# A transformer block's modulation weights with nine neighbouring rows per partition, and its condition vector loaded as columns

## The chip, the cores and the metric

One Trainium2 chip, one core. The metric is the device time of one execution in microseconds (us). "PE" is TensorE's matmul side, "DVE" VectorE, "ACT" ScalarE, "POOL" GpSimd, "SP" the engine that issues most loads.

## The reference

One block of a diffusion transformer: B = 2, 256 tokens each, D = 1152, all in bfloat16. What matters here is that a condition vector c (2 x 1152) is turned into six modulation vectors by one matmul with w_mod (1152 x 6912), and that layer norm of x does not need c.

```python
mod = (silu(c) @ w_mod).reshape(B, 6, 1, D)
shift_a, scale_a, gate_a, shift_m, scale_m, gate_m = [mod[:, i] for i in range(6)]
h = layernorm(x) * (1 + scale_a) + shift_a
qkv = (h @ wqkv).reshape(B, N, 3, H, Dh)
# ... attention, wo, second layernorm with scale_m / shift_m, gelu MLP ...
```

## The kernel before

The kernel is a list of operations that a scheduler written in Python puts in order per engine. PE and SP keep program order; for the start, ACT and DVE orders are fixed by hand. The parts that matter here:

```python
wmod_v = w_mod.rearrange("(k p) f -> p k f", p=P)      # row k*128+p on partition p
# loads of the head, in SP's order; c on ACT's queue
dma(CSB[0:18, :], c.rearrange("b (k p) -> (b k) p", p=P), ..., "ld_c", eng="act")   # 18 rows of 256 bytes
for b in range(2):
    dma(X[:, 2*b:2*b+2, :], xv[b], ...)                 # x0, x1: runs of 4608 bytes
for (ka, kb) in ((0, KC), (KC, KT)):                    # KC = 4, KT = 9
    for k0, k1 in ((0, 3), (3, 6), (6, 9)):             # scale columns: 3 + 3 loads, runs of 1024 / 1280 bytes
        dma(WSC[:, k0:k1, ka*P:kb*P], wmod_v[:, k0:k1, D+ka*P:D+kb*P], ...)
    for kt in range(ka, kb):
        dma(WK[:, kt, :], wqkv_v[:, kt, D:2*D], ...)
# ...
for i in range(5):                                       # warm-up matmuls
    mm(ps32(5), IDENT, Q4B, True, True)
tr(CT_PS, CSB[0:18, :], IDENT[0:18, 0:18])               # c rows -> columns on TensorE
act(... e.activation(out=TH, in_=CT_PS, func=Tanh, scale=0.5) ..., "c_tanh")
dve(... e.tensor_scalar(out=HC, in0=CT_PS, scalar1=0.5, op0=mult) ..., "c_half")
dve(... e.scalar_tensor_tensor(out=ST, in0=TH, scalar=1.0, in1=HC, op0=add, op1=mult) ..., "c_silu")
# ... first layer norm, its transposes, the first scale columns, the k projection of kt 0 to 3 (blocks of 128 of D's 1152) ...
for kt in range(KT):                                     # second scale columns: need the LAST of the six loads
    mod_kt(WSC, kt, 0, "scb_%d" % kt, (KC, KT))
sc1a(KC, KT)                                             # DVE copies those scales out of PSUM
# ...
S.first = {
    "dve": ["zq4b", "c_half", "c_silu", "bn_ln1_1_0", "bn_ln1_1_1", "bn_ln1_1_2", "aggr_ln1_1", "veps_ln1_1", "bn_ln1_2_0",
            "xn_1", ...],                                # c's work stands AHEAD of layer norm
    "act": ["ld_c", "c_tanh", "sum_ln1_0", "sq_ln1_0", ...],
}
```

Of the kernel before, what the change touches and what calls it, by code (L numbers as in the profile page):

```python
# [496 lines left out]
ALU = mybir.AluOpType  # L497
ACTF = mybir.ActivationFunctionType
AX = mybir.AxisListType

P = 128
# [43 lines left out]
def build_kernel(nc, x, c, wqkv, wo, w_mod, w_fc1, w_fc2, out):  # L545
    S = Sched()
# [4 lines left out]
    with (  # L551
# [4 lines left out]
        def sb(off, nbytes, dt=BF16):  # L556
            assert off % 4 == 0 and off + nbytes <= ARENA_BYTES, (off, nbytes)
            v = arena[:, off // 2:(off + nbytes) // 2]
            if dt == F32:
                v = v.bitcast(F32)  # L560
            return v

        def ps32(bank, c0=0, n=512):
            return psum[:, bank * 512 + c0: bank * 512 + c0 + n]

        def ps16(bank, c0=0, n=1024):
            v = psum[:, bank * 512: (bank + 1) * 512].bitcast(BF16)
            return v[:, c0:c0 + n]
# [15 lines left out]
        def misc(nbytes):  # L584
            o = mo[0]
            mo[0] += (nbytes + 3) // 4 * 4
            assert mo[0] <= ARENA_BYTES
            return o
# [41 lines left out]

        IDENT = sb(misc(256), 256)
        ONES = sb(misc(256), 256)
        CSB = sb(misc(256), 256)
        TH = sb(misc(72), 72, F32)
        HC = sb(misc(72), 72, F32)
        ST = sb(misc(36), 36)
# [26 lines left out]
        xv = x.rearrange("b (p t) d -> b p t d", t=2)  # L663
        outv = out.rearrange("b (p t) d -> b p t d", t=2)
        wqkv_v = wqkv.rearrange("(k p) f -> p k f", p=P)
        wmod_v = w_mod.rearrange("(k p) f -> p k f", p=P)
        wo_v = wo.rearrange("(k p) f -> p k f", p=P)
        wfc1_v = w_fc1.rearrange("(k p) f -> p k f", p=P)
        wfc2_v = w_fc2.rearrange("(k p) f -> p k f", p=P)
# [1 line left out]
        def dma(dst, src, nbytes, name, is_out=False, eng="sp", run=4096):  # L671
            eff = 0.95 if run >= 4096 else (1.0 if run >= 2304 else (1.08 if run >= 1536 else 1.14))
            return S.op(eng, 500.0 if eng == "sp" else 150.0, lambda e: e.dma_start(dst, src), reads=[src], writes=[dst],  # L673
                        name=name, dma_bytes=nbytes * eff, is_out=is_out)

        def dve(cost, fn, reads, writes, name):
            return S.op("dve", cost, fn, reads=reads, writes=writes, name=name)

        def act(cost, fn, reads, writes, name):
            return S.op("act", cost, fn, reads=reads, writes=writes, name=name)  # L680
# [10 lines left out]
        def mm(o, l, r, st, sp, **kw):  # L691
            S.instr(lambda e: e.matmul(o, lhsT=l, rhs=r, start=st, stop=sp, **kw), reads=[l, r], writes=[o])  # L692

        def tr(o, i_, idn):
            S.instr(lambda e: e.transpose(o, i_, idn), reads=[i_, idn], writes=[o])  # L695


        dma(CSB[0:18, :], c.rearrange("b (k p) -> (b k) p", p=P), 18 * 256, "ld_c", eng="act")
        for b in range(2):
            dma(X[:, 2 * b:2 * b + 2, :], xv[b], 2 * P * D * 2, "ld_x%d" % b)  # L700
        for (ka, kb) in ((0, KC), (KC, KT)):
# [22 lines left out]
        for i in range(5):  # L724
            S.unit("pe", 430.0, "warm_a%d" % i)
            mm(ps32(5), IDENT, Q4B, True, True)
        CT_PS = ps16(6, 0, 18)
        S.unit("pe", 100, "c_T")
        tr(CT_PS, CSB[0:18, :], IDENT[0:18, 0:18])
        act(200, lambda e: e.activation(out=TH, in_=CT_PS, func=ACTF.Tanh, scale=0.5), [CT_PS], [TH], "c_tanh")  # L730
        dve(170, lambda e: e.tensor_scalar(out=HC, in0=CT_PS, scalar1=0.5, scalar2=None, op0=ALU.mult), [CT_PS], [HC], "c_half")
        i3 = IDENT.rearrange("p (a i) -> p i a", a=4)
        dve(200, lambda e: e.tensor_reduce(out=QS, in_=i3, axis=AX.X, op=ALU.add), [IDENT], [QS], "qs")
        q4 = QS.unsqueeze(1).broadcast_to([P, 4, 32])
# [22 lines left out]
        for t in range(4):  # L757
# [3 lines left out]
            else:  # L761
# [3 lines left out]
                                                                                 op0=ALU.subtract, op1=ALU.mult),  # L765
# [480 lines left out]
        for t in range(4):  # L1246
            b = t // 2
# [48 lines left out]
def bass_standalone__dit_block__diffusion_kernel(  # L1296
    nc: bass.Bass,
    x: bass.AP,
    c: bass.AP,
    wqkv: bass.AP,  # L1300
    wo: bass.AP,
    w_mod: bass.AP,
    w_fc1: bass.AP,
    w_fc2: bass.AP,
    out: bass.AP,
):
    build_kernel(nc, x, c, wqkv, wo, w_mod, w_fc1, w_fc2, out)
# [28 lines left out]
```

## Time and profile before

| | before |
|---|---|
| time, median of 3 runs (range) | 245.71 us (245.51 to 245.8) |
| span of the profiled run | 243.9 us |
| PE busy | 239.0 us, 98% |
| PE's waits in the whole run | 1.5 us at the start, 0.4 us near 18.7 us |

From the page of the before kernel: busy time by engine, the DMA packets, the queue that carries c (q10), and the chain of work that ended last.

```profile
span 243.9 us, 4070 instructions
...
PE 239.0 (98%) x1755; PEld 147.4 (60%) x1755; DVE 120.9 (50%) x218; ACT 66.5 (27%) x134; POOL 21.3 (9%) x39
...
DMA packets 30140, 51.59 MB, mean 212 GB/s; under 512 B 1703, under 2 KB 15787, under 8 KB 30123
...
q10 hardware_dynamic: 27, 0.00, 0.0%
...
PE psum L692 90%; DMA arena<-in_w_mod_dram 5%; SPq L673 2%; PE psum L695 1%; DVE arena L1259 0%; DVE arena L1260 0%
```

The kernel is bound by PE; L692 is the helper that issues every matmul, L695 the one that issues transposes. The view of waits for PE, "who waited for whom, total us, times, longest":

```profile
PE psum L692 <- POOL arena L715: 1.5, 1, 1.5
PE psum L692 <- DMA arena<-in_w_mod_dram: 0.4, 1, 0.4
```

Those are all of PE's waits. The critical chain in order of time (start, length, what) shows where the second comes from:

```profile
7.11 11.57 DMA arena<-in_w_mod_dram
18.68 0.05 issue
18.73 40.89 PE psum L692 x310
```

A load of w_mod, the last of the six scale loads, is issued at 7.11 us and lands at 18.68; from then on the chain is PE work up to the last two DVE operations. So 0 to 18.7 us ("the head") is the one stretch where a load or c's path can move the time. The timeline of the head, cut to c's work and the first layer-norm work (start, length, engine, line, operation; in brackets the idle time before it and what ended it):

```profile
0.79 0.59 ACTq L673 DMA_DIRECT2D arena<-in_c_dram  x1
...
3.75 0.19 PE L695 MATMUL psum<-arena 18*128 18x18 bf16 x1
...
3.98 0.19 ACT L730 ACTIVATE arena<-psum 128x18 f32<-128x18 bf16 x1 [1.28 <-PE psum L695]
4.27 0.18 DVE L731 TENSOR_SCALAR arena<-psum 128x18 f32<-128x18 bf16 x1 [3.09 <-ACT arena L730]
...
4.41 1.16 ACT L751 ACTIVATE arena<-arena 128x1152 bf16<-128x1152 bf16 x1 [0.24 <-DMA arena<-in_x_dram]
4.49 0.18 DVE L736 SCALAR_TENSOR_TENSOR arena<-arena 128x18 bf16<-128x18 f32 x1
4.58 1.47 DVE L743 BATCH_NORM_STATS2 arena<-arena 128x6 f32<-128x384 bf16 x3
```

c's work (transpose, tanh L730, halving L731, product L736) ends 0.26 us after ACT has x at 4.41 us, so it costs layer norm at most 0.17 us. The load of c itself had landed by 2.2 us; its transpose stood behind warm-up matmuls in PE's order until 3.75. PE's timeline of the end of the head:

```profile
13.04 5.33 PE L692 MATMUL psum<-arena 128*128 128x256 bf16 x71
18.73 14.45 PE L692 MATMUL psum<-arena 128*128 128x2 bf16 x163 [0.35 <-DMA arena<-in_w_mod_dram]
```

PE starts its run of projections of kt 0 to 3 at 13.04 us, is through with what it can do at 18.37 and waits 0.35 us for the load. That is the slack of everything ahead of it on PE.

### The profile page before, as it was taken

The numbers are of one execution on the slowest core, as the hardware profiler recorded it, in microseconds if no ns is written. First come the engines' busy times: TensorE is split into PE (matmuls) and PEld (weight loads), VectorE is DVE, ScalarE is ACT, GpSimd is POOL, SyncE is SP. The second block draws the span as 40 slices with busy tenths as digits, with TensorE's granted clock in tenths as the row PEclk, the third lists the DMA queues.
The fourth block names the chain that finished last, engine by engine and source line by source line (L and its number), as shares of the span: only waits on it lengthen the run. The fifth ranks groups of instructions, "written<-read, shape, count | busy, mean of one in ns | idle before, by whom it ended". The sixth has DMA issues, their size and how long they took to land.

```text
span 243.9 us, 4070 instructions
## 1 busy us (share of the span) xinstructions
PE 239.0 (98%) x1755; PEld 147.4 (60%) x1755; DVE 120.9 (50%) x218; ACT 66.5 (27%) x134; POOL 21.3 (9%) x39
## 2 busy tenths in 40 slices
PE   7999999999999999999999999999999999999994
PEld 2698754556667666898444444444656565656584
DVE  3814398596997899689999500000022211111112
ACT  5730340345424206973233222223000000000000
POOL 1400000000021186400000000020000000000000
DMA  6999999999995999979953498030000000000000
GB/s 234 333 381 391 389 392 389 398 411 409 389 350 171 343 390 392 393 264 393 312 173 86 145 329 300 0 86 14 0 16 19 16 16 19 16 27 21 19 16 19
DMA packets 30140, 51.59 MB, mean 212 GB/s; under 512 B 1703, under 2 KB 15787, under 8 KB 30123
## 3 DMA queue, kind: packets, MB, share of 16 engines
q1 hardware_dynamic: 29680, 50.14, 57.5%
q0 software_dynamic: 416, 1.19, 1.6%
q8 instruction: 14, 0.23, 0.4%
q14 instruction: 3, 0.02, 0.0%
q10 hardware_dynamic: 27, 0.00, 0.0%
HBM read 50.14 MB, written 1.19 MB: 210 GB/s over the span
## 4 chain that ended last, share of the span: by engine, by line
PE 91%; DMA 5%; SPq 2%; issue 0%; DVE 0%
PE psum L692 90%; DMA arena<-in_w_mod_dram 5%; SPq L673 2%; PE psum L695 1%; DVE arena L1259 0%; DVE arena L1260 0%
## 5 line engine op out<-in xcount | busy, mean ns | idle before, releaser
L692 PE MATMUL psum<-arena 128*128 128x384 bf16 (+12 forms) x1666 | 235.8, 308 | 1.9 <-POOL arena L715 1.5
L692 PEld LDWEIGHTS psum<-arena 128*128 128x128 bf16 (+4 forms) x1666 | 142.2, 97 | 91.3 <-issue 4.7
L1054 DVE SCALAR_TENSOR_TENSOR arena<-arena 128x1152 f32<-128x1152 bf16 x32 | 44.7, 1413 | 0.6
L1259 DVE TENSOR_TENSOR arena<-psum,arena 128x384 f32<-128x384 f32 (+3 forms) x14 | 7.0, 500 | 68.0 <-PE psum L692 68.0
L1168 ACT ACTIVATE arena<-psum 128x512 bf16<-128x512 f32 (+1 forms) x44 | 22.4, 520 | 42.7 <-PE psum L692 42.7
L687 ACT ACTIVATE arena<-psum 128x512 bf16<-128x512 f32 (+6 forms) x35 | 19.0, 560 | 39.8 <-PE psum L692 39.1
L689 DVE CAST arena<-psum 128x512 bf16<-128x512 f32 (+3 forms) x14 | 8.9, 645 | 11.9 <-PE psum L692 11.9
L673 POOL DMA_DIRECT2D dit_scratch<-arena x3 | 1.8, 616 | 115.9 <-DVE arena L689 59.1
L1136 POOL TENSOR_TENSOR arena<-arena 128x384 f32<-128x384 f32 x12 | 10.9, 914 | 11.2 <-DVE arena L1135 9.6
L1081 DVE CAST arena<-psum 72x32 bf16<-72x32 f32 x1 | 0.2, 188 | 21.3 <-PE psum L692 21.3
L743 DVE BATCH_NORM_STATS2 arena<-arena 128x6 f32<-128x384 f32 (+1 forms) x18 | 9.5, 548 | 0.1
L1141 ACT ACTIVATE arena<-arena 128x1152 bf16<-128x1152 f32 x4 | 5.3, 1343 | 11.1 <-DVE arena L1140 11.1
L1135 DVE TENSOR_TENSOR arena<-psum,arena 128x384 f32<-128x384 f32 x12 | 6.5, 552 | 1.5 <-PE psum L692 1.4
L1260 DVE TENSOR_TENSOR arena<-arena 128x384 bf16<-128x384 f32 (+3 forms) x14 | 7.0, 501 | 0.5
L695 PE MATMUL psum<-arena 128*128 128x128 bf16 (+1 forms) x89 | 7.1, 219 | 0.0
L695 PEld LDWEIGHTS psum<-arena 128*128 128x128 bf16 (+1 forms) x89 | 5.8, 98 | 2.0 <-issue 0.8
L1158 ACT ACTIVATE arena<-psum,arena 128x128 bf16<-128x128 bf16 x16 | 6.0, 456 | 1.7 <-PE psum L695 1.1
L1155 DVE TENSOR_SCALAR arena<-psum,arena 128x128 bf16<-128x128 bf16 x20 | 5.4, 335 | 1.9 <-PE psum L695 1.9
L1061 DVE TENSOR_REDUCE arena<-arena 128x36 f32<-128x1152 f32 x4 | 5.4, 1346 | 0.0
L1058 DVE STREAM_TRANSPOSE arena<-arena 128x1152 f32<-128x1152 f32 x4 | 5.4, 1363 | 0.0
L984 ACT ACTIVATE arena<-psum,arena 128x256 bf16<-128x256 f32 x8 | 3.7, 472 | 1.3 <-PE psum L692 0.9
L980 DVE TENSOR_REDUCE arena<-psum 128x2 f32<-128x512 f32 x4 | 2.8, 689 | 1.8 <-PE psum L692 1.8
(47 smaller groups left out, 45.2 us busy)
## 6 DMA issues: line engine op xcount, KB each, us to landing
arena<-in_w_fc_dram SPq DMA_DIRECT2D x9, 1152.0 KB, 7.6
arena<-in_w_fc_dram SPq DMA_DIRECT2D x4, 2592.0 KB, 17.5
arena<-in_wqkv_dram SPq DMA_DIRECT2D x18, 288.0 KB, 10.2
arena<-in_w_mod_dram SPq DMA_DIRECT2D x3, 1728.0 KB, 20.2
arena<-in_w_mod_dram SPq DMA_DIRECT2D x3, 864.0 KB, 13.8
arena<-in_w_mod_dram SPq DMA_DIRECT2D x9, 288.0 KB, 10.5
arena<-in_wqkv_dram SPq DMA_DIRECT2D x1, 2592.0 KB, 16.6
arena<-in_wo_dram SPq DMA_DIRECT2D x1, 2592.0 KB, 24.4
```

The costliest lines, as they stand in the source:

```text
L673: return S.op(eng, 500.0 if eng == "sp" else 150.0, lambda e: e.dma_start(dst, src), reads=[src], writes=[dst], name=name, dma_bytes=nbyte ...
L687: act(c_act(n), lambda e: e.activation(out=dst, in_=src, func=ACTF.Copy), [src], [dst], name)
L689: dve(c_dve_psum16(n) if psum16 else c_dve_psum32(n), lambda e: e.tensor_copy(dst, src), [src], [dst], name)
L692: S.instr(lambda e: e.matmul(o, lhsT=l, rhs=r, start=st, stop=sp, **kw), reads=[l, r], writes=[o])
L695: S.instr(lambda e: e.transpose(o, i_, idn), reads=[i_, idn], writes=[o])
L743: dve(550, lambda e, s=s, o=o: e.bn_stats(out=o, in_=s), [s], [o], "bn_%s_%d" % (tag, ci))
L1054: dve(1270, lambda e, w=w, s=s, acc=acc: e.scalar_tensor_tensor(out=acc, in0=w, scalar=s, in1=acc, op0=ALU.mult, op1=ALU.add), [w, s, acc] ...
L1135: dve(550, lambda e, o=o, ga=ga, x1c=x1c: e.tensor_tensor(out=x1c, in0=o, in1=ga, op=ALU.mult), [o, ga], [x1c], "wo_t1_%d_%d" % (t, ci))
L1136: S.op("pool", 930, lambda e, xs=xs, x1c=x1c: e.tensor_tensor(out=x1c, in0=x1c, in1=xs, op=ALU.add), reads=[x1c, xs], writes=[x1c], name=" ...
L1168: act(c_act(ntok), lambda e: e.activation(out=dst, in_=o, func=ACTF.Gelu_apprx_tanh), [o], [dst], "gelu_%d_%d" % (f, tok0))
L1259: dve(c_dve_psum32(w), lambda e, o=o, gm=gm, t1=t1: e.tensor_tensor(out=t1, in0=o, in1=gm, op=ALU.mult), [o, gm], [t1], "fc2_t1_%d_%d" % ( ...
L1260: dve(c_dve_32(w), lambda e, t1=t1, x1c=x1c, ost=ost: e.tensor_tensor(out=ost, in0=t1, in1=x1c, op=ALU.add), [t1, x1c], [ost], "fc2_out_%d ...
```

## The change

Its intent: c comes onto the partitions directly, without a transpose on PE and its PSUM detour. For that, partition p must hold rows 9p to 9p+8 of w_mod, nine neighbours in DRAM, so that c's nine elements of a partition lie side by side too.

```diff
-        wmod_v = w_mod.rearrange("(k p) f -> p k f", p=P)
+        wmod_v = w_mod.rearrange("(p k) f -> p k f", p=P)
...
-        dma(CSB[0:18, :], c.rearrange("b (k p) -> (b k) p", p=P), 18 * 256, "ld_c", eng="act")
+        dma(CSB.rearrange("p (b k) -> p b k", b=2), c.rearrange("b (p k) -> p b k", p=P), 18 * 256, "ld_c", eng="act")
...
-        CT_PS = ps16(6, 0, 18)
-        S.unit("pe", 100, "c_T")
-        tr(CT_PS, CSB[0:18, :], IDENT[0:18, 0:18])
-        act(200, lambda e: e.activation(out=TH, in_=CT_PS, func=ACTF.Tanh, scale=0.5), [CT_PS], [TH], "c_tanh")
-        dve(170, lambda e: e.tensor_scalar(out=HC, in0=CT_PS, scalar1=0.5, scalar2=None, op0=ALU.mult), [CT_PS], [HC], "c_half")
+        act(200, lambda e: e.activation(out=TH, in_=CSB, func=ACTF.Tanh, scale=0.5), [CSB], [TH], "c_tanh")
+        dve(100, lambda e: e.tensor_scalar(out=HC, in0=CSB, scalar1=0.5, scalar2=None, op0=ALU.mult), [CSB], [HC], "c_half")
```

(The tile CSB shrinks from 256 to 36 bytes a partition.) Each load of w_mod still takes a slice of columns, so no two rows join into a longer run.

More of the change, by code (lines that the diff above doesn't have):

```diff
@@ L632, in build_kernel @@
         ONES = sb(misc(256), 256)
-        CSB = sb(misc(256), 256)
+        CSB = sb(misc(36), 36)
         TH = sb(misc(72), 72, F32)
```

## The prediction

> **What bounds the kernel now.** TensorE. The profiled span is 243.9 us and the page gives PE 239.0 us busy (98%). The chain that ended last is PE matmuls (L692) without a break from 18.73 us to 241 us. The view of waits gives PE two waits in the whole run: 1.5 us at the start and 0.35 us ending at 18.73 us, for a load of w_mod. Before that, the chain runs through SP's issues into an 11.57 us w_mod transfer issued at 7.11 us. So only in the head, 0 to 18.7 us, can loads or the c path move the time. There the DMA engines are full: the table by stretches shows a DMA share of 0.92 to 1.1 from 3 us on.
>
> **What the change does.**
> 1. w_mod rows go to partitions as nine neighbours instead of 128 apart. A load still takes column slices of a row, so runs stay 1024, 1280, 2304 and 4608 bytes and the packets stay as many. I expect the same packet times (medians 46, 57, 95 and 182 ns). The first 1024-byte loads run at about 280 GB/s (5 to 9 us), mean packet 54 ns against a median of 46; if neighbouring rows removed that tail, 1152 x 8 ns / 16 engines = 0.6 us of DMA time would go. I give that a small chance.
> 2. c: 18 packets of 256 bytes become 256 of 18 bytes. The old ones took 15 to 18 ns. At that price the new load needs about 256 x 17 / 16 = 0.27 us of every DMA engine, against 0.02 before, and pushes the load that PE awaits at 18.7 us by about 0.25 us (estimates). The Trainium skill ("DMA: Bandwidth & Descriptors", Specifications) says that transfers below 512 bytes miss line rate; no run shows yet what 18 bytes cost.
> 3. Removed: one transpose (0.19 us on PE) among warm-up matmuls. tanh started at 3.98 us, the halving at 4.27, the product at 4.49, VectorE's first layer-norm statistics at 4.58 us, although x had landed at 4.41. If c lands before 4 us, VectorE starts about 0.15 us earlier. But the same page (Queues, rings and completion order) says that an engine takes turns between rings packet by packet. c's 16 packets an engine could alternate with the x packets (178 ns and more) and land near 5 us. ACT and VectorE have the c work ahead of layer norm, so the statistics would start 0.5 to 1 us later. PE's slack is 0.35 us.
>
> **Sum.** A gain in the head beyond the 0.35 us wait is lost; a DMA delay shows fully. -0.1 (chance of faster rows, shorter chain) +0.25 (c packets) +0.1 (chance of a late c) gives about +0.2 us: 245.9 us, range 245.2 to 246.8. Faster by over 2%: 0.01; within 2%: 0.98; slower: 0.01.
>
> **What would show it.** Packets under 512 bytes rise by about 245; w_mod packet medians stay; PE's wait near 18.7 us remains or grows to 0.4 to 0.7 us, or tanh is late and PE's first 18 us shift; after it PE runs without a gap and takes the same 222 us to the last matmul.
>
> **What would make it wrong.** The row order changes HBM speed: PE's wait goes (at best -0.4 us), or new PE waits for w_mod appear up to 60 us, where DMA is full too. 18-byte packets cost several times 17 ns: +1 us and more. The instruction order on VectorE or ACT is made from modelled times; another order could open small PE waits anywhere.

## The result

The after kernel took 245.86 us (median of 4 runs, 245.81 to 245.99), the before kernel 245.74 us (4 runs, 245.51 to 245.8) beside it. The ratio is 1.0007, 95% interval 0.999 to 1.0025: the same. The prediction said 245.9, range 245.2 to 246.8.

The page after, the same lines as before; line numbers are lower by 3 from L731 on (L730 is now L727):

```profile
span 244.3 us, 4059 instructions
...
PE 238.5 (98%) x1744; PEld 147.1 (60%) x1754; DVE 120.9 (50%) x218; ACT 66.4 (27%) x134; POOL 21.2 (9%) x39
...
DMA packets 30385, 51.59 MB, mean 211 GB/s; under 512 B 1948, under 2 KB 16032, under 8 KB 30368
...
q10 hardware_dynamic: 272, 0.00, 0.1%
...
PE psum L692 92%; PE psum L695 2%; DMA arena<-in_c_dram 2%; DVE arena L740 1%; DVE arena L761 1%; POOL arena L744 0%; POOL arena L752 0%; DVE arena L806 0%; DVE arena L741 0%; DVE arena L1256 0%; ACT arena L727 0%; DVE arena L1257 0%; DVE a
```

There are 245 packets more, all under 512 bytes: c's 18 + 9 became 256 + 16 (data and semaphore writes). The w_mod load is gone from the chain, and c's load has come in. The view of waits for PE, after:

```profile
PE psum L692 <- POOL arena L715: 1.5, 1, 1.5
PE psum L692 <- DVE arena L741: 0.3, 1, 0.3
```

PE no longer waits for w_mod at all. Its other wait, for a layer-norm step (L741, the aggregation), ends at 6.97 us, well before the projections; in the second profile of this kernel (e8 below) it is absent. The critical chain of after in order of time:

```profile
0.79 3.92 DMA arena<-in_c_dram
4.74 0.23 ACT arena L727
5.01 0.06 issue
5.07 0.18 DVE arena L733
5.25 1.40 DVE arena L740 x3
6.68 0.25 DVE arena L741
...
7.19 0.58 POOL arena L744
7.79 0.58 DVE arena L761
```

The load of 4.5 KB now opens the chain: it is issued at 0.79 us and releases tanh at 4.74. The timeline of the head, after:

```profile
0.79 0.46 ACTq L673 DMA_DIRECT2D arena<-in_c_dram  x1
...
4.74 0.22 ACT L727 ACTIVATE arena<-arena 128x18 f32<-128x18 bf16 x1 [2.17 <-DMA arena<-in_c_dram]
4.74 0.18 DVE L728 TENSOR_SCALAR arena<-arena 128x18 f32<-128x18 bf16 x1 [3.55 <-DMA arena<-in_c_dram]
4.86 1.15 ACT L748 ACTIVATE arena<-arena 128x1152 bf16<-128x1152 bf16 x1
...
5.07 0.18 DVE L733 SCALAR_TENSOR_TENSOR arena<-arena 128x18 bf16<-128x18 f32 x1 [0.15 <-ACT arena L727]
5.17 1.47 DVE L740 BATCH_NORM_STATS2 arena<-arena 128x6 f32<-128x384 bf16 x3
```

The chain of c is shorter by a transpose, yet it ends 0.58 us later (product at 5.07 against 4.49), because ACT waits 2.17 us and DVE 3.55 us for c. Both have c's work ahead of layer norm in their fixed order, so the statistics start at 5.17 instead of 4.58. And PE's end of the head:

```profile
13.45 0.28 PE L695 MATMUL psum<-arena 128*128 128x128 bf16 x2
13.56 19.65 PE L692 MATMUL psum<-arena 128*128 128x256 bf16 x232
```

The projections start at 13.56, 0.52 us later, and run on without a gap: the load is there when PE comes to it. The packets of the trace say why c is late (start times in us; each row 18-byte packets of c as listed by the trace, which does not name the DMA engine). Packet times in this document and in its expectations are 0.3 us later than on the clock of the views, where c's first packet starts at 1.75 us before and at 2.85 after; the shift is the same in every run, so differences between packet times stand:

```
before: 18 c packets of 256 bytes   first start 2.06, last end 2.19; x's first packet 2.13
after: 256 c packets of 18 bytes    first start 3.16, last end 4.52; x's first packet 2.12
  starts in after: 3.641 3.650 3.658 3.666 3.686 | 3.821 3.830 3.838 3.846 3.865
  a packet of x lasts 0.178
```

The first row of starts comes back 0.180 us later, one x packet apart. An 18-byte packet lasts only 0.009 us. Until x's first load is through, the records alternate in this way, one of c and one of x; after that the rest of c follows in bursts.

### The profile page after: what moved, and what is told of

It is laid out like the page before. It is cut to its first block, busy times and chain, and to the rows that moved or that the text cites. A ratio compares the mean times of both kernels' runs of the same rounds, so it can differ in the third digit from the quotient of the medians.

```text
span 244.3 us, 4059 instructions
## 1 busy us (share of the span) xinstructions
PE 238.5 (98%) x1744; PEld 147.1 (60%) x1754; DVE 120.9 (50%) x218; ACT 66.4 (27%) x134; POOL 21.2 (9%) x39
## 4 chain that ended last, share of the span: by engine, by line
PE 94%; DVE 2%; DMA 2%; issue 1%; POOL 0%; ACT 0%; DVEq 0%
PE psum L692 92%; PE psum L695 2%; DMA arena<-in_c_dram 2%; DVE arena L740 1%; DVE arena L761 1%; POOL arena L744 0%; POOL arena L752 0%; DVE arena L806 0%; DVE arena L741 0%; DVE arena L1256 0%; ACT arena L727 0%; DVE arena L1257 0%; DVE arena L733 0%; DVE arena L796 0%; DVE arena L743 0%
## 5 line engine op out<-in xcount | busy, mean ns | idle before, releaser
L692 PE MATMUL psum<-arena 128*128 128x384 bf16 (+10 forms) x1656 | 234.8, 307 | 2.5 <-POOL arena L715 1.5
L695 PE MATMUL psum<-arena 128*128 128x128 bf16 x88 | 7.1, 219 | 0.1
L695 PEld LDWEIGHTS psum<-arena 128*128 128x128 bf16 x88 | 5.6, 98 | 1.8 <-DVE arena L761 0.9
```

Of the source, the lines that this page charges most:

```text
L692: S.instr(lambda e: e.matmul(o, lhsT=l, rhs=r, start=st, stop=sp, **kw), reads=[l, r], writes=[o])
L695: S.instr(lambda e: e.transpose(o, i_, idn), reads=[i_, idn], writes=[o])
```

## The experiments

**The theories.** *Late c*: the only thing that moves the time is c's late landing, which holds up layer norm; the row order does nothing. *Two effects*: the new rows speed the head's loads by about 0.5 us (in the after profile the last 1280-byte packet of the scale loads ended at 17.91 us, before at 18.48), and the late c eats the gain. *Small packets*: the DMA time of 256 packets is what costs. Four runs came first: each half of the change alone, and a reordering that hides the late c, on both kernels.

### e1_rows_only: the row order alone

```diff
 (on the before kernel; result wrong on purpose, since c stays in the old order)
-        wmod_v = w_mod.rearrange("(k p) f -> p k f", p=P)
+        wmod_v = w_mod.rearrange("(p k) f -> p k f", p=P)
```

> The before kernel with the new row order of w_mod alone; c stays in the old order, so the result is wrong on purpose. Late-c theory (the new rows do nothing; only the late c moves the time): 245.7 us, as before; the last 1280-byte packet of w_mod ends near 18.5 us and PE waits about 0.35 us near 18.7. Two-effects theory (the rows speed the head's loads by about 0.5 us and the late c eats it): the last 1280-byte packet ends near 17.9 to 18.0 us, PE's wait at 18.7 is gone, 245.3 to 245.4 us. Either way tanh stays at about 4.0 us.

Measured: 245.64 us (5 runs, 245.03 to 245.97), ratio to before 0.9996, interval 0.9982 to 1.0009. Wrong result. The last 1280-byte packet ended at 18.81 us, later than before. PE's wait in its view of waits:

```profile
PE psum L692 <- DMA arena<-in_w_mod_dram: 0.7, 1, 0.7
```

In this profile the new rows alone did not bring the load forward, which speaks against the two-effects theory. It does not settle it: the interval reaches down to 0.4 us faster, and one landing proves little, as the next runs show.

### e2_c_only: the c columns alone

```diff
 (on the after kernel; result wrong on purpose)
-        wmod_v = w_mod.rearrange("(p k) f -> p k f", p=P)
+        wmod_v = w_mod.rearrange("(k p) f -> p k f", p=P)
```

> The after kernel with the old row order of w_mod; result wrong on purpose. Both theories: tanh at about 4.7 us, first statistics near 5.2 us, 245.8 to 246.0 us. They differ in the load: two-effects theory has the last 1280-byte packet end at 18.5 us or later, so PE waits again at 18.7 to 18.9 us for about 0 to 0.2 us; late-c theory has it at 17.9 us as in the after run.

Measured: 245.93 us (245.42 to 246.02), ratio 1.0001, interval 0.9989 to 1.0014; wrong result. The halving started at 4.58 us and the statistics at 5.01, so c is late with the old rows too. The last 1280-byte packet ended at 18.76 us and PE waited 0.27 us for it. Neither theory's picture is complete: the load landed at 17.9 or 18.8 us without regard to the rows.

### e3_ln_first and e4_before_ln_first: layer norm ahead of c's work

```diff
-            "dve": ["zq4b", "c_half", "c_silu", "bn_ln1_1_0", "bn_ln1_1_1", "bn_ln1_1_2", "aggr_ln1_1", "veps_ln1_1", "bn_ln1_2_0",
+            "dve": ["zq4b", "bn_ln1_1_0", "bn_ln1_1_1", "bn_ln1_1_2", "aggr_ln1_1", "veps_ln1_1", "c_half", "bn_ln1_2_0", "c_silu",
                     "xn_1", ...
-            "act": ["ld_c", "c_tanh", "sum_ln1_0", "sq_ln1_0", ...
+            "act": ["ld_c", "sum_ln1_0", "c_tanh", "sq_ln1_0", ...
```

> The after kernel with ACT and VectorE doing the first layer-norm work before the c work, so that c's late landing is hidden. Statistics start at about 4.4 us and xn_T near 8.2 us. Late-c theory: 245.6 to 245.75 us, PE waits again for w_mod at 18.7 us. Two-effects theory: 245.3 to 245.4 us, no PE wait between 9 and 19 us above 0.1 us. If the small packets' DMA time were what costs, the time would stay at 245.9 us.

> The before kernel with the same reordering of ACT and VectorE. Both theories: no gain, 245.7 us, since PE has 0.35 us of slack to the w_mod load at 18.7 us; PE's wait there grows a little, to 0.35 to 0.5 us. If the layer-norm chain did bound the head, it would be 0.1 to 0.2 us faster.

Measured: on the after kernel 245.46 us (245.15 to 246.04), ratio to before 0.9993, interval 0.998 to 1.0007. On the before kernel 245.92 us (245.27 to 246.06), ratio 1.0008, interval 0.9995 to 1.0022. Both correct. DVE's timeline and PE's, of the after kernel with layer norm first:

```profile
4.44 1.48 DVE L740 BATCH_NORM_STATS2 arena<-arena 128x6 f32<-128x384 bf16 x3 [3.25 <-DMA arena<-in_x_dram]
```

```profile
13.08 5.33 PE L692 MATMUL psum<-arena 128*128 128x256 bf16 x71
18.62 11.57 PE L692 MATMUL psum<-arena 128*128 128x2 bf16 x138 [0.20 <-DMA arena<-in_w_mod_dram]
```

The statistics start as soon as x is there, PE's projections start at 13.08 (13.04 before the change), and the wait for w_mod is back. The late c is hidden, and the load ends the head again. The median lies below the 245.6 to 245.75 us that the late-c theory gave, but no gain over the before kernel can be told from noise. The profiled run of the latter had the load at 18.02 us and no wait for it, so its wait did not grow as I expected.

### e5_c_behind_x and e6_c_behind_x_ln_first: the suspected delay made larger

```diff
-        dma(CSB.rearrange("p (b k) -> p b k", b=2), c.rearrange("b (p k) -> p b k", p=P), 18 * 256, "ld_c", eng="act")
         for b in range(2):
             dma(X[:, 2 * b:2 * b + 2, :], xv[b], 2 * P * D * 2, "ld_x%d" % b)
+        dma(CSB.rearrange("p (b k) -> p b k", b=2), c.rearrange("b (p k) -> p b k", p=P), 18 * 256, "ld_c")     # on SP's queue
```

(e6 has the reordering of e3 as well; "ld_c" leaves ACT's list.)

> The after kernel with c's column load issued on SP's queue behind the two x loads, so that c lands later still. Late-c theory: the last c packet near 5.9 to 6.1 us, tanh near 6.2 us, statistics near 6.6 us, 2.0 us later than before the change; PE has about 0.35 us of slack to the w_mod load, so about 1.3 to 1.8 us slower than before: 247.0 to 247.6 us, with no PE wait for w_mod. If a late c did not matter: 245.7 to 246.0 us.

> The same late c, but with the first layer-norm work ahead of the c work on ACT and VectorE. Late-c theory: statistics back at 4.4 us, 245.3 to 245.9 us although c lands at 6 us. If it is the placing of c's packets or SP's extra issue that costs, the time stays near that of the run with c behind x and the old order.

Measured: e5 247.81 us (4 runs, 247.3 to 248.22), ratio 1.0084, interval 1.0065 to 1.0102, clearly slower. Its runs fall into two pairs: 247.3 and 247.4 us at a granted clock of 1.0 and 0.998, as the late-c theory expected, and 248.2 us twice at 0.993, above it. e6 246.31 us (4 runs, 245.95 to 246.35), ratio 1.002, interval 1.0007 to 1.0034. Both correct. DVE in e5:

```profile
6.12 0.18 DVE L728 TENSOR_SCALAR arena<-arena 128x18 f32<-128x18 bf16 x1 [4.93 <-DMA arena<-in_c_dram]
6.45 0.18 DVE L733 SCALAR_TENSOR_TENSOR arena<-arena 128x18 bf16<-128x18 f32 x1 [0.16 <-ACT arena L727]
6.55 1.47 DVE L740 BATCH_NORM_STATS2 arena<-arena 128x6 f32<-128x384 bf16 x3
```

The statistics start 1.97 us later than before the change, and the time of the profiled run is 1.66 us longer (247.30 against 245.64), the rest being taken up by PE's slack. With layer norm first, about two thirds of that come back (246.3 us) although c's packets lie in about the same place; that is still above the 245.9 us expected. The rest goes through ACT, whose tanh I had put second and which stood for c here, on the chain that ended last:

```profile
6.45 0.22 ACT L727 ACTIVATE arena<-arena 128x18 f32<-128x18 bf16 x1 [0.90 <-DMA arena<-in_c_dram]
```

### e7_more_small_packets: the price of a small packet

```diff
 (on e3; nobody reads DUM, a memset late on POOL waits for it; two more semaphores)
+        dv, cv = DUM.rearrange("p (k w) -> p k w", w=2)[:, :, 0], wqkv[0:P, 0:18]        # 128 x 18 packets of 2 bytes
+        S.op("act", 150.0, lambda e: e.dma_start(dv, cv, allow_slow_non_contiguous=True), ..., name="ld_dummy")
```

> The after kernel with layer norm first, plus one more load that nobody waits for in the head: 2304 packets of 2 bytes on ACT's queue behind c. It prices small packets. At the 9 ns that an 18-byte packet took in the after run it takes 2304 x 9 / 16 = 1.3 us of each DMA engine, all before the w_mod load that PE waits for at 18.7 us: 1.0 to 1.4 us slower than the run with layer norm first alone, so 246.5 to 247.0 us with a PE wait for w_mod of 1.2 to 1.6 us. At the 15 to 18 ns that my prediction used: 247.6 to 248.0 us. If small packets only fill gaps of the engines: no change, 245.3 to 245.9 us.

Measured: 248.27 us (4 runs, 247.1 to 249.87), ratio 1.0094, interval 1.0045 to 1.0142; correct. Two runs took 247.1 us at a granted clock of 1.0, close to the 246.5 to 247.0 us of the 9 ns theory; two took 249.4 and 249.9 at 0.993. The profile is of the 249.4 us run. The 2304 packets took a mean of 9.02 ns. Of the 1152 packets of the last three scale loads, the middle one ended 1.0 us later than in e3 and the 1050th 1.33 us later (17.71 against 16.38 us), about what 9 ns a packet says; but the very last ended 3.4 us later (21.79 against 18.39). The extra microseconds lie in the last hundred packets. In addition PE waited three times for w_mod and its clock fell. Two rows of the table by stretches (stretch, its length, then busy time and instructions of PE, PEld, DVE, ACT, POOL; granted clock; DMA share; GB/s):

```profile
10.00:12.00 2.00, 0.62 (x17) 0.50 (x16) 1.16 (x2) 1.30 (x2) 1.13 (x2) 1.00 1.04 357
...
14.00:16.00 2.00, 2.00 (x16) 1.63 (x15) 1.49 (x7) 1.50 (x3) 0.00 (x0) 0.50 1.07 356
```

PE was busy for 0.62 of 2 us, and two stretches later its clock was 0.50. So this run prices small packets at 9 ns of the mean engine, and shows that the last packets can lose more; it does not give one number for the kernel's time.

### e8_after_again and e9_before_again: the same kernels once more

No edit. They ask how much the landing of the load varies by itself.

> The after kernel unchanged, once more. If the landing of the last scale load varies from run to run by itself (theory: one DMA engine falls behind, not the row order), its last 1280-byte packet ends anywhere between 17.9 and 18.8 us, not at 17.9 us again by rule; 245.7 to 246.0 us, tanh at 4.5 to 4.8 us.

> The before kernel unchanged, as a control of the noise. Theory: before the change the head ends when the last scale load lands, and that landing varies by itself; after it, when PE's layer-norm chain is through. So the before kernel should spread more from run to run (245.2 to 246.0 us, as its nine runs beside the last experiments did) than the after kernel did (245.8 to 246.0), its tanh should be at about 4.0 us and its PE wait between 0 and 0.8 us. If it spreads no more than the after kernel, that part of the theory falls.

Measured: after 245.84 us (5 runs, 245.78 to 245.96), ratio to before 1.0005, interval 0.9993 to 1.0018. Before 245.63 us (5 runs, 245.39 to 245.75), ratio to the other runs of before 1.0002. In the after kernel the last 1280-byte packet ended at 17.42 us (17.91 the first time), below the range that I had expected, in the before kernel at 18.27 (18.48 the first time). Tanh of the after kernel came at 4.62 us. In the profiled run of e9 x landed later, the statistics started at 4.78 us, and PE had no wait for w_mod; so even the before kernel is not always held by the load. The spread of e9's own five runs (0.36 us) is narrower than the 0.8 us that I expected from the nine runs beside e5 to e8 (245.22 to 245.96), and wider than that of the after kernel (0.18 here).

### e10_ln_first_again: does the reordering win?

No edit to e3.

> The after kernel with layer norm ahead of the c work, once more, unchanged, to see whether its 245.46 us median beats the before kernel. Theory: with the late c hidden, the last scale load ends the head again, so it is the before kernel's time within noise and with the wide spread: median 245.4 to 245.8 us, PE wait 0 to 0.6 us for w_mod.

Measured: 245.54 us (5 runs, 245.35 to 245.7), beside 245.56 us of before; ratio 1.0001, interval 0.9988 to 1.0015. In its profile PE did not wait for the load, so layer norm, and not the load as the theory had it, ended the head. The reordering hides the late c and wins nothing. No version of mine beat the before kernel.

### e11_c_before_x: why c is late

```diff
-        dma(CSB..., c.rearrange("b (p k) -> p b k", p=P), 18 * 256, "ld_c", eng="act")
+        dma(CSB..., c.rearrange("b (p k) -> p b k", p=P), 18 * 256, "ld_c")        # SP's queue, ahead of x
```

> The after kernel with c's column load issued on SP's queue ahead of the x loads. It asks why c is late. If c's packets are late because x's packets stand before and between them: the first c packet starts near 2.1 us, the last ends before 2.8 us, tanh before 3.2 us; x lands about 0.45 us later (one more issue) at 4.8 us, statistics at 4.8 to 4.9 us, time 245.6 to 245.9 us. If 256 small packets are late by themselves (their making takes a microsecond more): the first packet stays near 3.1 us and x is held up behind it by a microsecond, statistics after 5.3 us, 245.9 to 246.6 us.

Measured: 246.45 us (5 runs, 246.3 to 246.71), ratio 1.0037, interval 1.0024 to 1.0049; correct. c's packets ran from 2.18 to 2.51 us, all 256 in 0.33 us, and c landed 1.8 us after its issue. So 256 small packets are not late by themselves; they are late where x's packets stand before and between them. The run also moved c to SP's queue. No run has the 256 packets on ACT's queue without x beside them, so why their first packet starts 1.1 us later there than the 18 old ones did stays open. My time was wrong, though: x's first packet started at 2.70 instead of 2.12 us, and x0 landed at 5.59 (views' clock) instead of 4.5, about 1.1 us later and not the 0.45 us of one more issue. Time and statistics are those that the other theory gave; where the rest of x's delay comes from is not shown.

```profile
1.29 4.30 DMA arena<-in_x_dram
...
5.62 1.48 DVE L740 BATCH_NORM_STATS2 arena<-arena 128x6 f32<-128x384 bf16 x3 [2.52 <-DMA arena<-in_x_dram]
```

Layer norm waits for x now, at 5.62 us. Putting c first moves the delay from c to x.

### One sum that fits the runs

From the profiles: S is the start of the first statistics, K the start of PE's projections of kt 0 to 3, L the end of the last 1280-byte scale packet, C the start of DVE's copy of the second scales, T the time of that same run.

| run | S | K | L | C | T | T - C |
|---|---|---|---|---|---|---|
| before | 4.58 | 13.04 | 18.48 | 19.42 | 245.64 | 226.2 |
| before again (e9) | 4.78 | 13.41 | 18.27 | 19.55 | 245.63 | 226.1 |
| rows only (e1) | 4.58 | 12.97 | 18.81 | 19.72 | 245.92 | 226.2 |
| before, layer norm first (e4) | 4.45 | 13.09 | 18.02 | 19.23 | 245.27 | 226.0 |
| after | 5.17 | 13.56 | 17.91 | 19.70 | 245.99 | 226.3 |
| after again (e8) | 5.05 | 13.43 | 17.42 | 19.57 | 245.84 | 226.3 |
| c only (e2) | 5.01 | 13.39 | 18.76 | 19.69 | 245.95 | 226.3 |
| after, layer norm first (e3) | 4.44 | 13.08 | 18.39 | 19.31 | 245.15 | 225.8 |
| the same again (e10) | 4.45 | 13.08 | 17.71 | 19.22 | 245.35 | 226.1 |
| c behind x (e5) | 6.55 | 14.94 | 17.94 | 21.08 | 247.30 | 226.2 |
| c behind x, layer norm first (e6) | 4.29 | 13.91 | 17.71 | 20.05 | 246.27 | 226.2 |
| c before x (e11) | 5.62 | 14.25 | 19.24 | 20.39 | 246.52 | 226.1 |

In all twelve, C is within 0.03 us of the larger of K + 6.14 and L + 0.92 (before: 18.48 + 0.92 = 19.40; after: 13.56 + 6.14 = 19.70), and everything behind C takes 225.8 to 226.3 us. (L is on the packets' clock; on that of the views the constant is 1.23.) Two chains race to the same place: layer norm through PE, and the scale load. e7 is left out, since its earlier waits and its clock break the first chain.

## Why the prediction was right, and where its sum was not

The number held: +0.2 us was forecast, 245.9 us, and the medians differ by 0.12 us. In means, all 36 runs of the before kernel give 245.68 us and all 9 of the after kernel 245.86, a difference of 0.18 us; they come from several chips, and no interval of runs taken side by side excludes zero, so the size of the loss is not shown, only that it is a few tenths at most. The steps:

1. *PE bounds the kernel, only the head can move the time, and the rest takes the same time.* Right. T - C varies by 0.5 us over all twelve profiles, C by 1.9 us, and T follows C.
2. *The row order does nothing to the loads.* Right, as far as can be told. The median packets of w_mod stayed at 46, 55 to 59 and 93 to 96 ns in the first 45 us (1024, 1280 and 2304 bytes, by load), and rows alone gave a ratio of 0.9996. With c in its usual place, 1050 of the 1152 packets of the last scale loads had ended at 16.22 to 16.42 us with old rows and at 16.10 to 16.40 with new. L scatters more: 17.42 to 18.81 with new rows, 18.02 to 18.76 with old. Its earlier value in the after profile, which tempted me into the two-effects theory, fits another source (see below).
3. *c's packets cost 0.27 us of every DMA engine and push the load by 0.25 us.* This term failed. An 18-byte packet took 9 ns, not the 15 to 18 ns of a 256-byte packet, so the term is 256 x 9 / 16 = 0.14 us. Nor can it be seen: L was earlier in both profiles of after than in both of before, and its own scatter is several times larger. It was on the wrong side of the race as well: with c late, the load has slack.
4. *A late c, given only +0.1 us as a chance.* This is what happened, in every profile with columns on ACT's queue and the old order: c's work started at 4.58 to 4.74 us, and the statistics 0.43 to 0.59 us later than the 4.58 us of the first before profile (0.23 to 0.39 later than the 4.78 of e9). The alternation with x's packets was in the text, and so was the slack of 0.35 us. In the first pair of profiles K moved by 0.52 us, of which the wait for the load absorbed about half: C moved by 0.28 us. In the second pair (e9 and e8) K and C moved by only 0.02, since x was late in e9.

So +0.25 for packets and +0.1 for a late c should have been about 0 and, by C of the two profiles of each kernel, +0.02 to +0.28. The two errors cancel: that the sum came out right is luck, and a forecast of no change would have lain in the stated range too. The removed transpose was worth nothing: it stood among warm-up matmuls, and its chain was not on the path to layer norm by more than 0.17 us.

Why the load's last packets scatter can be read from the traces, though no run tested it. In the before profile 1050 of the 1152 packets had ended at 16.42 us and the last at 18.48. A 16 KB instruction fetch of 1.1 us starts between 15.7 and 17.9 us in the twelve profiles of the table. In each of them one long packet of SP's queue starts 14 or 15 ns before the fetch ends: 151 to 164 ns for 1280 bytes (the median is 55), or 254 to 255 ns for 2304 (median 95). In nine profiles it belongs to the scale load, and from there to L the load's last packets, 22 in the before profile and 2 in the after profile, run one after another. In e5, e6 and e8 it belongs to a later load. The reading: one DMA engine stands still for the fetch, and L depends on how many scale packets it still has to do. The trace does not name the engines, so this rests on the times alone, and why the fetch starts when it does stays open. Open too is why the clock was 0.993 in two runs of e5 and of e7.

The Trainium skill carried two steps. "DMA: Bandwidth & Descriptors" (Why a DMA increments its semaphore by 16 and not by 1) says that one descriptor moves one contiguous run of the last dimension: the trace has 256 packets of 18 bytes, one for each partition and batch. The same page (Queues, rings and completion order) says that an engine takes turns between queue rows: the starts that come back after 180 ns agree. Where c alone had the engines, in e11, its packets took 0.33 us in all; taking turns with x they took 1.36.

## What to carry to other kernels

A tiny load can open the critical chain: here 4.5 KB cut into 256 short runs, issued beside x's load, landed at 4.7 us, about when the first half of x did (4.5). Before taking out an operation that reshapes data on an engine with slack, ask what the new access pattern does to the landing time, and what stands behind it in the fixed order of each engine. Where two chains race to one point, a gain on one is worth no more than its lead over the other; and compare the landing in two profiles of the same kernel before explaining a difference of half a microsecond.

## What the Trainium skill lacked or had wrong

- "DMA: Bandwidth & Descriptors" (Specifications) gives 512 bytes as the least size for line rate; a price per small packet stands on the page (Bandwidth) only for a load issued from GpSimd. Here, issued from ACT, packets of 18 and of 2 bytes took 9 ns and packets of 256 bytes 15 to 18 ns; 2304 of the 2-byte ones delayed a later load by 1.0 us in its middle, and its last packet by 3.4 us.
- The same page (Queues, rings and completion order) has an engine drain a packet of typically 9 to 17 descriptors before it turns to another row. Here one 18-byte record of c alternates with one 178 ns record of x while both have work, as the starts 180 ns apart show. What is missing is the consequence: 4.5 KB landed 3.9 us after issue beside x, and 1.8 us after issue ahead of it (on SP's queue).
- The same page names two DMA engines that are often slower, with a guess at the cause that concerns loads issued from GpSimd. Here loads issued from SP had a tail of 2 us as well (1050 of 1152 packets at 16.42 us, the last at 18.48), and it varied from run to run by 1.4 us. The times point to an instruction fetch of 1.1 us that holds one engine; no page says what such a fetch costs a data load.
- No page says whether neighbouring rows in DRAM make a load faster when the runs stay as long. Here they did not: 0.9996, interval 0.9982 to 1.0009.
- "TensorE: Matmul & The Clock Gate" (Why this matters for your kernels) warns of PE gaps over about 3 us. In e7 the clock fell to 0.50 in the stretch 14 to 16 us, after three waits of 0.4, 1.4 and 0.4 us between 9.0 and 13.1 us. Another section of the page (A second HAM failure mode: psum-queue depth-cycling) tells of frequent short gaps, but gives no length for them.
